# Hash attention with a feed-forward block: the order of VectorE's work between two pairs of heads, and how the second pair's q and k are turned

## Chip, cores and metric

The kernel runs on one core of a Trainium2 chip. The metric is the device time of one execution in microseconds (us). The engines are named as in the profile: PE is TensorE (matmuls; PEld its weight loads), DVE is VectorE, ACT is ScalarE, POOL is GpSimd, SP is SyncE, which only issues DMAs here.

## The reference

Inputs are q, k, v of shape (4 batches, 8 heads, 768 positions, 64), a projection of 64 x 6, and a feed-forward block of 512 x 2048 and 2048 x 512 with a slope alpha per hidden unit. For each batch and head:

```
bucket(q), bucket(k) = the 6 sign bits of q @ proj and of k @ proj
scores = q @ k.T / 8, and -1e9 where bucket(q) != bucket(k)
attn   = softmax(scores) @ v
```

The heads are put beside each other to x (3072 x 512), and the result is

```
h = x @ w_in;  g = max(h, 0) + alpha * min(h, 0);  out = g @ w_out
```

## The kernel before

**Stages.** The function `fast_path` has two stages. The attention stage works on 16 pairs of heads (`NPAIR`; two heads fill the 128 partitions), one after the other, and in its shadow converts the feed-forward weights, which come as 64-bit floats, to 32-bit ones, 32 pieces of 128 x 512, two for each pair. The feed-forward stage then runs blocks of seven products each with sums and differences on DVE. Nearly all compute instructions go through `do`, which pins them to the order of the program on their engine, so the order in the source is the order on each engine; an instruction that waits holds up all behind it. DMAs that are not wrapped in `do` may be placed among these by the framework.

**One pair on PE.** `scores(pi, ...)` makes 12 cells: each is four matmuls into a tile `sc` of two PSUM banks (the hash bits `qb`, `kb` in bf16, then `qT`, `kT` in f32), and ACT's exponential (L770) writes it to `pt`. `hash_bits(pi + 1)` then makes the next pair's bits (`hs`, ACT's sign L735, and six small DMAs from POOL, L740 and L742). `attend(pi)` multiplies `pt` by v into `av` (L800), 96 matmuls. `totals(pi)` multiplies the summed probabilities `accd` by ones into `sm` (L814), 16 matmuls. `sc`, `hs`, `sm` and the transposes `tp_q`, `tp_k` share a ring of three PSUM tiles (`two_banks`), so the third score cell of a pair takes the tile that `sm` had, when `st` has read it.

**One pair on DVE.** `add_first` (L778) sums the first two probability tiles into `accp` as soon as four exponentials are there. For the pair before come `dn` (L842) and `x` (L848), the end of `divide`. Then follow one weight's `weight_sum` (L637, L640), `weight_clamp` (L606) for the next weight, `add_third` (L786), `add_last` (L782, L783), the second weight's `weight_parts` (L612) and `weight_sum` (L637, L640), and `add_total` (L789), which adds `accp` to `accd`. Then the q and the k of pair pi + 2 are turned, in three of the pairs with a subtraction for the feed-forward block (L873) behind them, and `divide(pi)` begins: `st` (L830, two transposes of `sm`), `rc`, `rr` (L831, L833, reciprocals), `vs` (L840), and, through `weight_begin`, `weight_clamp` and `weight_parts` of the next weight and `add_first` of the next pair.

**How q and k are turned.** Pairs 2 to 15 are loaded by blocks (`load_blocks`, L512: four DMAs of 96 KB in rows of 128 B from SP for each tile), so that a 32 x 32 block transpose on DVE (`turn_blocks`, L703) gives `qT` and `kT`; ACT scales q (L1197). Pairs 0 and 1 are loaded whole (`load_part`, L501, rows of 256 B), turned by PE with an identity (`turn`, L694, six transposes each), and copied out of PSUM by ACT (q, with the scale, L699) and DVE (k, L697). The source tiles `qn` and `kn` have three buffers, `qT` and `kT` two.

**Weights.** ACT's two conversions (`weight_abs`, L596 to `wr` and L600 to `wx`) fill two buffers that `weight_sum` frees. POOL makes four differences for every four pieces (`weight_sums`, L658), each 1.27 us; a small copy of one column of `accd` (L675, `late_sum`) stands ahead of one of them and makes it wait for that tile.

Of the kernel before, what the change touches and what calls it, by code (L numbers as in the profile page):

```python
# [12 lines left out]
AF = mybir.ActivationFunctionType  # L13
# [394 lines left out]
def fast_path(  # L408
# [12 lines left out]
    nc = tc.nc  # L421
# [15 lines left out]
    DOWN = 2.0 ** -20  # L437
# [5 lines left out]
    do = tc.keep_in_program_order  # L443
    PE, DVE, ACT, POOL = nc.tensor, nc.vector, nc.scalar, nc.gpsimd
# [10 lines left out]
    NPAIR = len(pairs)  # L455
# [24 lines left out]
    nat, tr, bits = {}, {}, {}  # L480
    accp, accd, av, vsum, sums = {}, {}, {}, {}, {}

    def load(pi, name):
        b, hp = pairs[pi]
        src = {"q": q, "k": k, "v": v}[name]
        if name == "v":
            t = pool.tile([P, 2, NC * D], F32, name=f"vn{pi}", tag="vn")
            nc.sync.dma_start(t, src[b, 2 * hp : 2 * hp + 2].rearrange("h (p c) d -> p h (c d)", c=NC))
            nat[name, pi] = t
        elif pi > 1 and name in BY_BLOCKS:  # L490
            load_blocks(pi, name)
        else:
            load_part(pi, name, slice(0, NC), nc.sync)

    def load_part(pi, name, cs, queue):
        b, hp = pairs[pi]
        src = {"q": q, "k": k}[name]
        if cs.start == 0:
            nat[name, pi] = pool.tile([P, NC, 2, D], F32, name=f"{name}n{pi}", tag=f"{name}n", bufs=3)
        for s in range(2):  # L500
            queue.dma_start(nat[name, pi][:, cs, s], src[b, 2 * hp + s].rearrange("(p c) d -> p c d", c=NC)[:, cs])  # L501

    BY_BLOCKS = 'qk'

    def load_blocks(pi, name):
        b, hp = pairs[pi]
        src = {"q": q, "k": k}[name]
        nat[name, pi] = t = pool.tile([P, NC * 4, 32], F32, name=f"{name}n{pi}", tag=f"{name}n", bufs=3)
        for s in range(2):
            for h in range(2):  # L510
                a = D * s + 32 * h
                nc.sync.dma_start(  # L512
                    t[a : a + 32].rearrange("i (c u) d -> i c u d", u=4),
                    src[b, 2 * hp + s, :, 32 * h : 32 * h + 32].rearrange("(u i c) d -> i c u d", u=4, c=NC),
                )
# [62 lines left out]
    def load_weight(i):  # L578
        if i < NW:
            i = order[i]  # L580
            raw[i] = pool.tile([P, 512], moe_w_in.dtype, name=f"raw{i}", tag="raw", bufs=3)
            nc.sync.dma_start(raw[i], piece(i))
# [19 lines left out]
    def weight_clamp(i):  # L602
        if i < NW:
            i = order[i]
            x = wx[i]
            do(DVE.tensor_scalar(x, x, HI_MIN, None, op0=ALU.max, op1=ALU.max, accum_out=wmax[:, i : i + 1]))  # L606

    def weight_parts(i):
        i = order[i]
        x = wx[i].bitcast(U32)  # L610
        turned = i < HW and i % 4 == 3
        do(DVE.tensor_scalar(  # L612
            x, x, 3, 0x40000000 if turned else 0xC0000000, op0=ALU.logical_shift_left, op1=ALU.bitwise_xor,
        ))
# [55 lines left out]
    late_sum = const.tile([P, 1], F32, name="late_sum")  # L670

    def weight_sums(count, after=None):

        if sums_due and after is not None:
            do(POOL.tensor_copy(late_sum, after[:, 0, :1]))  # L675
        while sums_due and count:
            fn, x = sums_due.pop(0)
            count -= fn.__name__ == "one"
            fn(*x)


    def two_banks(name):
        return psum.tile([P, 2, 512], F32, name=name, tag="sc", bufs=3)

    BOTH = slice(0, 2)

    def turn(pi, name, halves=BOTH, engine=None):

        src = nat[name, pi].rearrange("p c h d -> p c (h d)")
        if halves.start == 0:  # L690
            tr[name, pi] = pool.tile([P, S], F32, name=f"{name}T{pi}", tag=f"{name}T")
        ps = two_banks(f"tp_{name}{pi}")
        for c in range(CH * halves.start, CH * halves.stop):
            do(PE.transpose(ps[:, c // CH, c % CH * P :][:, :P], src[:, c], ident))  # L694
        dst = tr[name, pi].rearrange("p (h w) -> p h w", h=2)[:, halves]
        if engine is DVE:
            do(DVE.tensor_copy(dst, ps[:, halves, :CW]))  # L697
        else:
            do(ACT.activation(dst, ps[:, halves, :CW], AF.Copy, scale=DOWN if name == "q" else 1.0))  # L699

    def turn_blocks(pi, name):
        tr[name, pi] = pool.tile([P, S], F32, name=f"{name}T{pi}", tag=f"{name}T")
        do(DVE.transpose(tr[name, pi], nat[name, pi].rearrange("p w d -> p (w d)")))  # L703
# [55 lines left out]
    def scores(pi, cells):  # L759
        for kc, g in cells:  # L760
            sc = two_banks(f"sc{pi}_{kc}_{g}")
            ks = slice(kc * P, (kc + 1) * P)
            qs = slice(g * CW, (g + 1) * CW)
            for what, first in ((bits, True), (tr, False)):
                for s in range(2):
                    r = slice(D * s, D * s + D)
                    do(PE.matmul(  # L767
                        sc[:, s, :CW], what["k", pi][r, ks], what["q", pi][r, qs], start=first, stop=not first,
                    ))
            do(ACT.activation(pts[kc][:, g, :, :CW], sc[:, :, :CW], AF.Exp, scale=SCALE / DOWN))  # L770


    def p(kc):
        return pts[kc].rearrange("p g s w -> p (g s) w")[:, :, :CW]

    def add_first(pi):
        accp[pi] = pool.tile([P, 2 * NCH, CW], F32, name=f"accp{pi}", tag="accp", bufs=1)
        do(DVE.tensor_tensor(accp[pi], p(0), p(1), op=ALU.add))  # L778

    def add_last(pi):  # L780
        accd[pi] = pool.tile([P, 2 * NCH, CW], F32, name=f"accd{pi}", tag="accd", bufs=1)
        do(DVE.tensor_tensor(accd[pi], p(3), p(4), op=ALU.add))  # L782
        do(DVE.tensor_tensor(accd[pi], accd[pi], p(5), op=ALU.add))  # L783

    def add_third(pi):
        do(DVE.tensor_tensor(accp[pi], accp[pi], p(2), op=ALU.add))  # L786

    def add_total(pi):
        do(DVE.tensor_tensor(accd[pi], accd[pi], accp[pi], op=ALU.add))  # L789
# [351 lines left out]
    for half in (first, second):  # L1141
        turn(0, "q", half)
        turn(0, "k", half, DVE)
        if half is first:
            nil[0]()
            hash_bits(0, first, DVE)
    load(1, "q")
    load(1, "k")
    load_weight(0)
    load(0, "v")  # L1150
    for i in range(1, 3):
        load_weight(i)
# [4 lines left out]
    ahead = [(kc, 0) for kc in range(CH)]  # L1157
    scores(0, ahead)
    hash_bits(0, second, DVE)
    turn(1, "q")  # L1160
    turn(1, "k", BOTH, DVE)

    weight_abs(0, DVE)
    weight_clamp(0)
# [1 line left out]
    for pi in range(NPAIR):  # L1166
        i = 2 * pi

        def weight_begin():
            weight_clamp(i)  # L1170
            weight_parts(i)
            add_first(pi)

        scores(pi, [c for c in CELLS if pi or c not in ahead])
        if pi:
            divide(pi - 1, weight_begin)
        else:
            add_first(pi)
        weight_sum(i)
        weight_group(i)  # L1180
        load_weight(i + 3)
        if pi == 0:
            weight_abs(1, DVE)
        weight_clamp(i + 1)
        add_third(pi)
        add_last(pi)
        weight_parts(i + 1)
        weight_sum(i + 1)
        weight_group(i + 1)
        load_weight(i + 4)  # L1190
        add_total(pi)
        if pi + 1 < NPAIR:
            hash_bits(pi + 1)
        weight_sums(1, accd[pi])
        if pi + 1 < NPAIR:
            if pi:
                do(ACT.activation(tr["q", pi + 1], tr["q", pi + 1], AF.Copy, scale=DOWN))  # L1197
        if pi + 2 < NPAIR:
            for name in "qk":
                (turn_blocks if name in BY_BLOCKS else turn)(pi + 2, name)  # L1200
        attend(pi)
        if pi + 1 == NPAIR:
            now = ff1(0, 0)
            now.step(1)
        totals(pi)
        if pi + 1 == NPAIR:
            now.step(5)
            divide(pi)
        else:
            weight_abs(i + 2)  # L1210
        if pi + 2 < NPAIR:
            load(pi + 2, "v")
        if pi in (9, 11, 15):
            load_w((9, 11, 15).index(pi))
        if pi in (9, 10, 12):
            load_x(0, *{9: (0,), 10: (2, 3), 12: (1,)}[pi])
        if 11 <= pi < 14 or pi == 15:
            sum_x(0, min(pi - 11, 3), DVE)
        if pi == 1:
            setup_alpha()  # L1220
        for name in "qk":
            magnitude(pi, name)
            if pi + 3 < NPAIR:
                load(pi + 3, name)
        if pi + 1 < NPAIR:
            weight_abs(i + 3)
# [97 lines left out]
```

## Time and profile before

| | us |
|---|---|
| median of 3 runs (880.39 to 883.41) | 880.72 |
| the profiled execution | 881.48 |
| its span, first to last instruction | 879.7 |

| engine | busy, us | share of the span | instructions |
|---|---|---|---|
| PE | 865.7 | 98% | 5718 |
| DVE | 745.3 | 85% | 1214 |
| ACT | 370.0 | 42% | 654 |
| POOL | 96.2 | 11% | 212 |

The attention stage takes the first 330 us or so, the feed-forward stage the rest. From 40 to 330 us PE is busy 285.18 of 290 us, DVE 262.09, ACT 219.71. TensorE's granted clock is 0.999 of full speed. A line of the timeline reads: start (us from the span's start), length, engine, line of the kernel, operation, output<-inputs, shape, count; in brackets is the idle time of the engine before it, and what ended it. A wait is put down to the event that came last.

### The profile page before, as it was taken

The page shows a single profiled execution, that of the slowest core. Times are in us where ns is not written, and L with a number is a line of the kernel's source. Part 1 is how long each engine was busy: PE and PEld are TensorE (multiplying, and loading weights), DVE is VectorE, ACT ScalarE, POOL GpSimd, SP SyncE. Part 2 cuts the span into 40 slices and gives each one's busy share as a digit, 9 for nine tenths or more (in the row PEclk, how much of TensorE's full clock was granted, in tenths as well). Part 3 has the DMA queues.
Part 4 walks back from the last instruction along what each step waited for, and adds up shares of the span by engine and source line. Part 5 has one row for each costly group of instructions (what it writes and reads, how often), then busy time and mean ns, then how long its engine had stood idle before and what let it go on. Part 6 is the DMA issues. An engine that isn't in the chain of part 4 may idle for free.

```text
span 879.7 us, 15201 instructions
## 1 busy us (share of the span) xinstructions
PE 865.7 (98%) x5718; PEld 576.0 (65%) x5718; DVE 745.3 (85%) x1214; ACT 370.0 (42%) x654; POOL 96.2 (11%) x212
## 2 busy tenths in 40 slices
PE   9999999999999999999999999999999999999996
PEld 4444444444444445559996558996557997557996
DVE  5999988999999878899897769898668989668986
ACT  7877788888877652221112222112222112222111
POOL 1221322213313301120000000000000000000000
PEclk9999999999999999999999999999999999999999
DMA  8866797798897617685433425334434433520242
GB/s 205 182 144 138 182 217 179 143 236 224 204 260 161 212 42 263 207 301 222 139 129 88 172 88 200 112 119 119 141 122 155 140 119 91 184 85 1 96 152 68
DMA packets 167682, 137.22 MB, mean 156 GB/s; under 512 B 122880, under 2 KB 151248, under 8 KB 164016
## 3 DMA queue, kind: packets, MB, share of 16 engines
q1 hardware_dynamic: 160000, 123.64, 49.9%
q0 software_dynamic: 5184, 11.34, 3.9%
q10 hardware_dynamic: 2416, 1.18, 0.5%
q8 instruction: 47, 0.77, 0.4%
q14 instruction: 35, 0.29, 0.1%
HBM read 104.87 MB, written 28.31 MB: 151 GB/s over the span
## 4 chain that ended last, share of the span: by engine, by line
PE 66%; DVE 19%; issue 5%; DMA 4%; ACT 3%; SPq 1%; DVEq 0%; ACTq 0%
PE sc L767 3%; ACT pt L770 3%; DVE accd L789 3%; PE f_0a L901 2%; PE z_4a L901 2%; PE z_7a L901 2%; PE z_3a L901 2%; PE z_6a L901 2%; PE z_5a L901 2%; PE f_4a L901 2%; PE f_3a L901 2%; PE f_2a L901 2%; PE f_1a L901 2%; DVE accd L782 2%; DVE accp L786 2%
## 5 line engine op out<-in xcount | busy, mean ns | idle before, releaser
L770 ACT ACTIVATE pt<-sc 128x768 f32<-128x768 f32 x192 | 155.0, 811 | 37.0 <-PE sc L767 37.0
L767 PE MATMUL sc<-qT,kT 64*128 64x384 f32 x768 | 155.2, 482 | 0.0
L800 PE MATMUL av<-pt,vn 128*32 128x385 f32 (+1 forms) x1536 | 127.4, 486 | 0.0
L800 PEld LDWEIGHTS av<-pt,vn 128*32 128x32 f32 x1536 | 48.8, 109 | 77.4 <-issue 68.0
L767 PEld LDWEIGHTS sc<-qT,kT 64*128 64x128 f32 x768 | 68.2, 187 | 37.8 <-issue 36.4
L954 DVE TENSOR_TENSOR g<-g,g 128x384 f32<-128x384 f32 x128 | 68.4, 555 | 2.2
L767 PE MATMUL sc<-qb,kb 64*128 64x384 bf16 x384 | 63.3, 323 | 1.7 <-DVE st L830 1.4
L1018 DVE TENSOR_TENSOR gs<-g,gs 128x768 f32<-128x768 f32 x56 | 53.3, 952 | 1.0
L1010 DVE TENSOR_TENSOR ws<-wl 128x512 f32<-128x512 f32 x56 | 38.5, 687 | 18.4 <-DMA wl<-w_out_s 16.1
L1018 DVE TENSOR_TENSOR gs<-g 128x768 f32<-128x768 f32 x56 | 53.3, 952 | 0.0
L778 DVE TENSOR_TENSOR accp<-pt,pt 128x1536 f32<-128x1536 f32 x16 | 28.3, 1770 | 21.2 <-ACT pt L770 21.2
L740 POOL DMA_DIRECT2D qb<-kb x60 | 30.1, 505 | 136.0 <-ACT kb L735 114.8
L950 DVE SCALAR_TENSOR_TENSOR g<-h,alpha 128x384 f32<-128x384 f32 x32 | 19.7, 616 | 25.2 <-ACT h L943 25.1
L767 PEld LDWEIGHTS <-kb 64*128 64x128 bf16 x384 | 19.0, 94 | 31.6 <-DVE st L830 5.3
L596 ACT ACTIVATE wr<-raw 128x512 int32<-128x512 uint32 x32 | 22.5, 703 | 26.8 <-issue 19.5
L783 DVE TENSOR_TENSOR accd<-accd,pt 128x1536 f32<-128x1536 f32 x16 | 28.1, 1759 | 1.7
L786 DVE TENSOR_TENSOR accp<-accp,pt 128x1536 f32<-128x1536 f32 x16 | 28.0, 1753 | 0.0
L782 DVE TENSOR_TENSOR accd<-pt,pt 128x1536 f32<-128x1536 f32 x16 | 28.0, 1752 | 0.0
L789 DVE TENSOR_TENSOR accd<-accd,accp 128x1536 f32<-128x1536 f32 x16 | 28.0, 1751 | 0.0
L901 PE MATMUL f_0a<-x,wi 128*128 128x384 f32 x64 | 23.5, 489 | 0.0
L901 PE MATMUL f_4a<-x,wi 128*128 128x384 f32 x64 | 23.3, 486 | 0.0
L901 PE MATMUL f_1a<-x,wi 128*128 128x384 f32 x64 | 23.3, 486 | 0.0
(353 smaller groups left out, 1742.8 us busy)
## 6 DMA issues: line engine op xcount, KB each, us to landing
wi<-w_in_s SPq DMA_DIRECT2D x32, 896.0 KB, 4.7
wl<-w_out_s SPq DMA_DIRECT2D x16, 1024.0 KB, 4.8
wl<-w_out_r SPq DMA_DIRECT2D x12, 1024.0 KB, 5.1
raw<-in_moe_w_out_dram SPq DMA_DIRECT2D x16, 512.0 KB, 4.6
raw<-in_moe_w_in_dram SPq DMA_DIRECT2D x16, 512.0 KB, 4.3
w_in_s<-wsi SPq DMA_DIRECT2D x16, 448.0 KB, 6.3
vn<-in_v_dram SPq DMA_DIRECT2D x16, 384.0 KB, 5.2
x_s<-x SPq DMA_DIRECT2D x16, 384.0 KB, 2.6
```

Source lines behind the costliest of these rows:

```text
L740: nc.gpsimd.dma_start(bits["q", pi][D * s : D * s + 32, cols], raw[c + 32 : c + 64, 2 * half])
L767: do(PE.matmul(sc[:, s, :CW], what["k", pi][r, ks], what["q", pi][r, qs], start=first, stop=not first,))
L770: do(ACT.activation(pts[kc][:, g, :, :CW], sc[:, :, :CW], AF.Exp, scale=SCALE / DOWN))
L778: do(DVE.tensor_tensor(accp[pi], p(0), p(1), op=ALU.add))
L782: do(DVE.tensor_tensor(accd[pi], p(3), p(4), op=ALU.add))
L786: do(DVE.tensor_tensor(accp[pi], accp[pi], p(2), op=ALU.add))
L789: do(DVE.tensor_tensor(accd[pi], accd[pi], accp[pi], op=ALU.add))
L800: do(PE.matmul(av[pi][D * s + t : D * s + t + 32, g, :w], nat["v", pi][:, s, kc * D + t : kc * D + t + 32], pts[kc][:, g, s, :w], start=(k ...
L901: do(PE.matmul(self.ps[bank], self.left(left, k), self.right(right, k), start=start and k == 0, stop=k == self.nk - 1, skip_group_check=no ...
L954: do(DVE.tensor_tensor(new_g(b, to)[:, i], g_m[b, x][:, i], g_m[b, y][:, i], op=ALU.subtract))
L1010: do(DVE.tensor_tensor(t, w2[b, n, x], w2[b, n, y], op=op))
L1018: do(DVE.tensor_tensor(t, g2[b, n, x], g2[b, n, y], op=ALU.subtract))
```

## The change

- `add_total(pi)` stands directly behind `add_last(pi)`, ahead of the second weight's `weight_parts` and `weight_sum`.
- Of the two turns at the end of a pair only q's stays; k's turn of pair pi + 1 stands in `weight_begin`, so behind the reciprocals and `vs` of `divide(pi - 1)` and ahead of `weight_clamp`.
- POOL's delayed weight difference waits for `qT` of pair pi + 2 instead of `accd`, and in the last two pairs for nothing.
- Pair 1 is loaded by blocks and turned by DVE like the later ones: q's four DMAs come from SP, k's four from POOL. ACT's scaling of q now happens for pair 1 too, with its own instruction.

On the engines this means: PE has 12 transposes less. The first of POOL's four new DMAs stands between the two instructions that make the identity, the other three behind POOL's memsets. On DVE the copy L697 of pair 1 becomes two instructions of L703.

```
@@ load
-        elif pi > 1 and name in BY_BLOCKS:
+        elif pi and name in BY_BLOCKS:
@@ load_blocks
-    def load_blocks(pi, name):
+    def load_blocks(pi, name, queue=nc.sync):
...
-                nc.sync.dma_start(
+                queue.dma_start(
@@ weight_sums
-            do(POOL.tensor_copy(late_sum, after[:, 0, :1]))
+            do(POOL.tensor_copy(late_sum, after[:, :1]))
@@ the start
-    load(1, "k")
+    load_blocks(1, "k", nc.gpsimd)
...
-    turn(1, "q")
-    turn(1, "k", BOTH, DVE)
+    turn_blocks(1, "q")
+    turn_blocks(1, "k")
@@ the loop over the pairs
         def weight_begin():
+            if pi + 1 < NPAIR:
+                turn_blocks(pi + 1, "k")
             weight_clamp(i)
...
         add_last(pi)
+        add_total(pi)
         weight_parts(i + 1)
         weight_sum(i + 1)
         weight_group(i + 1)
         load_weight(i + 4)
-        add_total(pi)
         if pi + 1 < NPAIR:
             hash_bits(pi + 1)
-        weight_sums(1, accd[pi])
-        if pi + 1 < NPAIR:
-            if pi:
-                do(ACT.activation(tr["q", pi + 1], tr["q", pi + 1], AF.Copy, scale=DOWN))
+            do(ACT.activation(tr["q", pi + 1], tr["q", pi + 1], AF.Copy, scale=DOWN))
         if pi + 2 < NPAIR:
-            for name in "qk":
-                (turn_blocks if name in BY_BLOCKS else turn)(pi + 2, name)
+            turn_blocks(pi + 2, "q")
+            weight_sums(1, tr["q", pi + 2])
+        else:
+            weight_sums(1)
         attend(pi)
```

## The prediction

> **What bounds the kernel now.** I read the page first, for the engine that is never free.
>
> ```profile
> PE 865.7 (98%) x5718; PEld 576.0 (65%) x5718; DVE 745.3 (85%) x1214; ACT 370.0 (42%) x654; POOL 96.2 (11%) x212
> ```
>
> TensorE (PE) has 14 us of idle time in all, so the change can gain little: it must take PE's waits away, or PE's work. The table of waits of PE names them (total us, times, longest):
>
> ```profile
> PE sm L814 <- DVE accd L789: 3.4, 14, 0.3
> PE sc L767 <- DVE st L830: 1.4, 3, 0.5
> ```
>
> Both lie in the attention stage and both are VectorE (DVE) arriving late. The timeline shows one of the 14 (start, us, engine, line, out<-in, count):
>
> ```profile
> 93.74 1.76 DVE L778 TENSOR_TENSOR accp<-pt,pt 128x1536 f32<-128x1536 f32 x1 [1.38 <-ACT pt L770]
> ...
> 104.53 3.42 PE L800 MATMUL av<-pt,vn 128*32 128x384 f32 x40
> 107.12 0.13 PEld L800 LDWEIGHTS av<-pt,vn 128*32 128x32 f32 x4 [0.19 <-issue]
> 106.28 1.75 DVE L789 TENSOR_TENSOR accd<-accd,accp 128x1536 f32<-128x1536 f32 x1
> 107.95 0.97 DVE L703 STREAM_TRANSPOSE qT<-qn 128x768 f32<-128x768 f32 x1
> 108.18 0.86 PE L814 MATMUL sm<-accd,ones 128*32 128x192 f32 x16 [0.23 <-DVE accd L789]
> 108.97 0.34 PE L767 MATMUL sc<-qb,kb 64*128 64x384 bf16 x2
> 113.33 1.76 DVE L778 TENSOR_TENSOR accp<-pt,pt 128x1536 f32<-128x1536 f32 x1 [1.39 <-ACT pt L770]
> ```
>
> This is a closed loop: from L778 to the end of L789 14.29 us of DVE work without a wait (93.74 to 108.03), 0.15 to the sums' first matmul, 0.79 to the next scores, 4.36 until ScalarE (ACT) has the fourth exponential: 19.59 us, the period. So DVE's chain, not PE's work, sets the period. Pair 0 is the control:
>
> ```profile
> 25.56 4.38 PE L800 MATMUL av<-pt,vn 128*32 128x384 f32 x52
> 27.64 1.75 DVE L789 TENSOR_TENSOR accd<-accd,accp 128x1536 f32<-128x1536 f32 x1
> 29.12 0.13 PEld L800 LDWEIGHTS av<-pt,vn 128*32 128x32 f32 x4 [0.19 <-issue]
> 29.76 0.84 PE L814 MATMUL sm<-accd,ones 128*32 128x192 f32 x16
> 30.53 0.34 PE L767 MATMUL sc<-qb,kb 64*128 64x384 bf16 x2
> ```
>
> Its accd is ready at 29.39, 0.37 before sm. From the last weight load of av to sm it takes 0.64 us; in the pair above 1.06. A wait of 0.23 thus costs 0.42, since the overlap with av's tail is lost too.
>
> **What the Trainium skill says.** "TensorE: Matmul & The Clock Gate", section "Step-by-step: what each phase is for": only weight loads are pulled ahead, matmuls stay in program order. The trace agrees: the 16 matmuls of sm hold up the next pair's scores behind them. "DMA: Bandwidth & Descriptors", section "Issuing engines are not separate DMA queues": DMAs of all issuers share the same 16 engines and interleave. It agrees: from 2 to 4 us ACT's queue took 62.1% of them and SP's 43.3%.
>
> **Part 1: L789 moves ahead of L612, L637, L640.** These three take 1.79 us (first start 45.58, L789's start 47.37 in pair 1). accd is ready 1.79 us earlier, 1.4 us or more ahead of need; 14 waits go. Per pair 0.42, less 0.02 (sm to scores is 0.77 in pair 0, 0.79 here): 14 x 0.40 = **-5.6 us**. Upper bound 0.46 (pair 0's weight load of sm, idle 0.26 before it, may itself have lost 0.07), lower 0.24 (the plain wait). What is late next: PE's own work, since DVE keeps about 1 us of its 1.38 idle per pair. Behind L789 stand the weight's second pass and, waiting for it, ACT's second weight conversion: it began at 204.38, right after L640, and left ACT idle 2.30 before the first exponential at 208.00. With L640 1.67 later and scores 0.40 earlier, 2.30 - 1.67 - 0.40 leaves 0.23 us. I count zero; the score ring of three banks covers some half a microsecond more (first exponential 0.81, fourth cell 2.4 after the first). SP's raw load for that slot issues 1.7 later with the loads behind it; the weight is read in the next pair and v's loads later still: zero.
>
> **Part 2: k's turn moves behind the reciprocals.** In pairs 11 to 13 a subtraction for x (L873) also stands ahead of st:
>
> ```profile
> 246.81 0.92 DVE L873 TENSOR_TENSOR x<-x,x 128x768 f32<-128x768 f32 x1
> 247.64 0.64 DVE L830 STREAM_TRANSPOSE st<-sm 128x192 f32<-128x192 f32 x2
> 248.34 0.34 PE L767 MATMUL sc<-qb,kb 64*128 64x384 bf16 x2 [0.47 <-DVE st L830]
> ```
>
> The third score cell needs the bank that st frees; these periods are 20.23 instead of 19.58 (sm at 225.70, 245.28, 265.51). kT's pitch ahead of st is 0.86 (245.95 to 246.81); st comes that much earlier, scores 0.40: 0.86 - 0.40 = 0.46 of the 0.65 goes, 3 x 0.46 = **-1.4 us** (bounds 0.9 and 2.0). k's 0.9 us now fall where DVE waited 1.38 for ACT: free, and its first reader (the hash at the end of the scores) is 8 us away. If that cover were gone it would push L778 by up to 0.9. Its data was loaded a pair earlier, so no DMA wait is added. GpSimd's weight difference now waits for qT, about 0.9 later than before relative to the pair's sums; it takes 1.27 and rr's copies 0.9, and dn needs them only 4 us on: zero.
>
> **Part 3: pair 1 by VectorE.** Gone: 12 transposes of PE and a copy of 0.81 on ACT, and DVE's copy of 0.96; added: two DVE turns (0.97 + 0.94) and a scaling on ACT (0.84) later, where ACT is idle. The transposes cost PE little:
>
> ```profile
> 12.10 0.88 PE L694 MATMUL tp_q<-ident,qn 128*128 128x128 f32 x6
> 12.25 1.17 ACT L748 ACTIVATE qb<-hsq,hb 32x384 bf16<-32x384 f32 x2
> 13.81 0.34 PE L767 MATMUL sc<-qb,kb 64*128 64x384 bf16 x2 [0.17 <-DVE kb L754]
> 14.28 0.68 ACT L596 ACTIVATE wr<-raw 128x512 int32<-128x512 uint32 x1
> ```
>
> The next scores need both qb, done at 13.42, so only 13.81 - 13.42 = 0.4 can be gained. Against it stand the loads. By blocks a tile is 3072 packets of 128 B instead of 1536 of 256 B. From 18 to 20 us (128 B) 1517 packets took 90.3% of 16 engines, 19.0 ns each; from 6 to 8 us (256 B) 1428 took 78.5%, 17.6 ns. A tile takes 3.65 instead of 1.69 us, both +3.9. Free DMA time from 4 to 8 us is 0.36 x 2 + 0.215 x 2 = 1.15. k comes over GpSimd (POOL): 8 DMAs of 512 rows took 759 ns, 60 of 32 rows 505, so 768 rows are about 0.9 each. The first is placed between ident's two instructions (ident 1.32 to 2.2, needed at 4.38: covered), three after the memsets, to 6.4. The first meets q's and k's first halves, which PE awaits at 4.38 (bounds 0 and 0.8, I take 0.5), the others q's second half, awaited at 7.47 (same bounds, 0.5). The qb of above then ends at 14.4. The first weight (issued 7.91, landing 4.9 later, 12.8) lands between 12.8 and 12.8 + 3.9 - 1.15 = 15.6; ACT's wr stands ahead of the next exponential, which moves from 14.87 to 15.1 or, at worst, 16.3. Three banks of scores absorb part: **+0.5 us** (bounds -0.4 and +2.0). On DVE the two turns end about 16.5 and accd of pair 0 about 29.0, against a need at 30: covered.
>
> **Sum.** -5.6 - 1.4 + 0.5 = -6.5. The profiled execution took 881.48 (span 879.7 and 1.8 around it): 875.0 after. It stood 0.76 above the median of 880.72, so the median becomes **874.2 us**. The feed-forward stage keeps its instructions and shifts.
>
> **Rivals.** (a) PE regains only the plain waits, 3.4 + 1.4, and the start costs 1.5: 877.4. For it: 0.42 rests on one pair as control. Against: that pair has the same instructions. Chance 0.11. (b) ACT becomes the loop: its margin of 0.23 is thin, and if the second conversion is some 1 us later than worked out, 0.3 of each pair's 0.40 is lost: -6.5 + 14 x 0.3 = -2.3, 878.4. Against: its input landed early in all but one pair. 0.05. (c) Slower: k of pair 1 lands late from GpSimd's queue. DVE is in order; the turn of k stands ahead of all weight and sum work of pair 0. Landing by 15.6 is free, to 16.8 absorbed by accd's slack, from there each microsecond delays the end by one; past 23.3 the gain is gone. Issued by 6.4, with the longest landing of this queue before (11.9) it would be 18.3, 875.7. To end at 886 it must land near 28. For it: no such short rows on this queue in this trace. Against: its 1536 B packets took as long as the others' of that size. 0.05. (d) That L789 isn't moved where the diff says: the program order is pinned on each engine and the built order shows it ahead in all pairs; nil.
>
> **Numbers.** The main case, 0.79, spans 880.7 - 8.8 = 871.9 (14 x 0.46 + 3 x 0.65 + 0.4) to 880.7 - 5.0 = 875.7. With (a) the range is 871.9 to 877.4. About 0.5% (4.4 us, below 876.3) can be told from no change: faster 0.79, same 0.16 (a, b), slower 0.05.
>
> **What would show it.** Right: no wait of sm for accd; sm some 0.64 after av's last weight load; periods near 19.2, of pairs 11 to 13 near 19.4; kT between vs and the clamp with DVE's idle before L778 near 1.0; scores at 14 to 14.5 after qb, not after kb. Wrong: idle of ACT's exponentials put down to ACT itself; DVE's first turn idle on a DMA of kn; PE's first transposes after 5.2; periods still at 19.5.

## The result, and the profile after

| | before | after |
|---|---|---|
| median of 13 runs each, us | 881.15 (880.24 to 883.41) | 878.43 (877.71 to 881.05) |
| ratio, 95% interval | | 0.9970 (0.9961 to 0.9979) |

The change gained 0.3%, 2.7 us; 874.2 was predicted, and 878.43 lies outside the range of 871.9 to 877.4. The profiled execution of after took 881.05 (span 879.3), 2.6 above its median; near pair 12 it has a wait of 2.7 us, shown below.

The page of after, busy time, share and instructions of each engine:

```profile
PE 863.8 (98%) x5706; PEld 576.9 (66%) x5706; DVE 757.9 (86%) x1215; ACT 366.9 (42%) x654; POOL 99.4 (11%) x215
```

PE has its 12 transposes less. The odd entry is DVE: 12.6 us more than before for one instruction more. The two turns of pair 1 in place of a copy are about 1 us of it (0.97 + 0.94 - 0.96). Most of the rest lies in two lines that the change doesn't touch: L831 takes 8.6 us in all instead of 2.8, L612 18.9 instead of 13.6. The table of PE's waits (total us, times, longest):

```profile
PE sc L767 <- ACT pt L770: 2.7, 1, 2.7
PE sc L767 <- DVE st L830: 2.2, 4, 1.3
...
PE sc L767 <- ACT qb L748: 1.0, 2, 0.7
```

The 14 waits of `sm` for `accd` are gone, as predicted. The waits for `st` were to shrink from 1.4 us, and grew to 2.2; the first line is a new wait. DVE's own table shows what the additional busy time was paid with. Before:

```profile
DVE accp L778 <- ACT pt L770: 21.2, 16, 2.0
```

After:

```profile
DVE accp L778 <- ACT pt L770: 7.6, 8, 2.3
```

Before, DVE was idle here in every pair, 1.3 us on average; now it is in half of them. The timeline of after from 86 us, in the same pair as in the prediction, shows where it went:

```profile
87.42 0.84 PE L814 MATMUL sm<-accd,ones 128*32 128x192 f32 x16
...
87.73 0.97 DVE L703 STREAM_TRANSPOSE qT<-qn 128x768 f32<-128x768 f32 x1
...
88.62 0.60 DVE L830 STREAM_TRANSPOSE st<-sm 128x192 f32<-128x192 f32 x2
...
88.98 1.27 POOL L658 TENSOR_TENSOR wsi<-wsi 128x512 f32<-128x512 f32 x1
...
89.26 1.01 DVE L831 TENSOR_SCALAR rc<-st 128x12 f32<-128x12 f32 x1
...
91.45 0.64 DVE L606 TENSOR_SCALAR_CACHE_REDUCE wx<-wx 128x512 f32<-128x512 f32 x1
...
91.72 1.28 POOL L658 TENSOR_TENSOR wsi<-wsi 128x512 f32<-128x512 f32 x1
...
92.14 1.14 DVE L612 TENSOR_SCALAR wx<-wx 128x512 uint32<-128x512 uint32 x1
...
93.20 1.75 DVE L778 TENSOR_TENSOR accp<-pt,pt 128x1536 f32<-128x1536 f32 x1
```

L831 handles 12 numbers a partition and took 0.17 us before; here it takes 1.01 and ends at 90.27, just when GpSimd's weight difference ends (88.98 + 1.27 = 90.25). L612 took 0.42 and takes 1.14 beside the second difference. Together this is 1.56 us, and L778 now starts with no idle before it. The second meeting has no edit of GpSimd behind it: L612 now stands behind k's turn, and so runs later; in k_back below, with that turn back, it takes 0.42 everywhere. In the kernel before, the first difference ran beside transposes and the second, after L612, in DVE's idle time:

```profile
88.74 1.28 POOL L658 TENSOR_TENSOR wsi<-wsi 128x512 f32<-128x512 f32 x1
...
89.27 0.93 DVE L703 STREAM_TRANSPOSE kT<-kn 128x768 f32<-128x768 f32 x1
...
90.12 0.60 DVE L830 STREAM_TRANSPOSE st<-sm 128x192 f32<-128x192 f32 x2
...
90.76 0.17 DVE L831 TENSOR_SCALAR rc<-st 128x12 f32<-128x12 f32 x1
...
91.93 0.43 DVE L612 TENSOR_SCALAR wx<-wx 128x512 uint32<-128x512 uint32 x1
...
92.49 1.27 POOL L658 TENSOR_TENSOR wsi<-wsi 128x512 f32<-128x512 f32 x1
```

The Trainium skill describes this, and the prediction missed it: "SBUF — State Buffer", section "Who interferes with whom", says that VectorE and GpSimd share one pair of ports as an exclusive lock, that `tensor_scalar` in its two-port modes (not the form with an accumulator) and operations with two SBUF inputs contend for it, that the later one blocks for the whole instruction of the other, and that an operation with one SBUF input outside these modes doesn't. What this case shows agrees: `tensor_scalar` L831 0.17 to 1.01, until the difference ends; transposes of 0.93 and 0.60 beside a difference, no longer than elsewhere; L606, the accumulating form, 0.64 although the second difference starts beside it, and that difference its usual 1.28. Operations with two SBUF inputs are held up in the experiments below. In which mode an instruction ran, no trace shows.

The starts of the sums (L814 in the timeline) give the periods. The differences (16 in all, two in each of eight pairs) come in two pairs running, here from 87.42 to 125.83; the periods from 87.42 on are 19.14, 19.27 and 19.71 (before, 19.59 each). I read this so: DVE falls behind by what its idle time doesn't pay; the lead of `accd` over `sm` covers it at first, and the third period pays. From 242.14 on they are 20.58, 24.11 and 19.15. The 24.11 holds the other new wait:

```profile
267.21 0.67 ACT L596 ACTIVATE wr<-raw 128x512 int32<-128x512 uint32 x1 [7.57 <-DMA raw<-in_moe_w_out_dram]
...
268.34 3.12 ACT L770 ACTIVATE pt<-sc 128x768 f32<-128x768 f32 x4
...
269.19 0.34 PE L767 MATMUL sc<-qb,kb 64*128 64x384 bf16 x2 [2.74 <-ACT pt L770]
```

One raw weight (512 KB) lands at 267.2, and the exponentials stand behind its conversion. Its load was issued at 259.49 and took 7.6 us; from 242 to 262 us the packets fill 1.00 of the 16 DMA engines' time. In the kernel before (0.96 in the same stretch) the same load was issued at 258.57, landed 5.65 us later, at 264.22, and was converted from 264.33 in an idle stretch of ACT. So the computing around the load comes 2.8 us earlier (sums at 262.72 instead of 265.51), the issue does not, and this execution's transfer is 2 us slower on top.

### The profile page after: what moved, and what is told of

Read it like the earlier page. It is cut to its first block, busy times and chain, and to the rows that moved or that the text cites. A ratio compares the mean times of both kernels' runs of the same rounds, so it can differ in the third digit from the quotient of the medians.

```text
span 879.3 us, 15198 instructions
## 1 busy us (share of the span) xinstructions
PE 863.8 (98%) x5706; PEld 576.9 (66%) x5706; DVE 757.9 (86%) x1215; ACT 366.9 (42%) x654; POOL 99.4 (11%) x215
## 4 chain that ended last, share of the span: by engine, by line
PE 67%; DVE 11%; issue 3%; ACT 2%; DMA 2%; SPq 0%; DVEq 0%; ACTq 0%
PE sc L767 4%; PE av L800 4%; PE f_0a L901 2%; PE z_4a L901 2%; PE z_7a L901 2%; PE z_3a L901 2%; PE z_6a L901 2%; PE z_5a L901 2%; PE f_4a L901 2%; PE f_2a L901 2%; PE f_1a L901 2%; PE f_3a L901 2%; PE z_2a L901 2%; PE f_5a L901 2%; PE z_1a L901 2%
## 5 line engine op out<-in xcount | busy, mean ns | idle before, releaser
L770 ACT ACTIVATE pt<-sc 128x768 f32<-128x768 f32 x192 | 153.1, 811 | 6.0 <-PE sc L767 5.2
L778 DVE TENSOR_TENSOR accp<-pt,pt 128x1536 f32<-128x1536 f32 x16 | 28.1, 1754 | 7.6 <-ACT pt L770 7.6
L901 PE MATMUL f_0a<-x,wi 128*128 128x384 f32 x64 | 23.5, 489 | 0.0
L901 PE MATMUL f_1a<-x,wi 128*128 128x384 f32 x64 | 23.3, 486 | 0.0
L901 PE MATMUL f_2a<-x,wi 128*128 128x384 f32 x64 | 23.3, 486 | 0.0
```

The lines of the kernel that those rows point to most:

```text
L901: do(PE.matmul(self.ps[bank], self.left(left, k), self.right(right, k), start=start and k == 0, stop=k == self.nk - 1, skip_group_check=no ...
```

## Experiments

Three theories. **A**: GpSimd's differences hold up VectorE; the change put them there. **C**: the DMA queue can't follow, and a raw weight arrives late near pair 12. **E**: the parts of the change are not worth the figures that they were given: with part 1 alone the wait only moves on to `st`, or the start (part 3) costs more. (B and D in the expectations are the rivals of A and C.) For each experiment the median of its 4 to 21 runs, the range and the ratio to the kernel before on the same chip are given. Three chips were used, one for each group; the medians of before were 881.10, 881.14 and 881.63.

### diff_shifted: the differences moved beside transposes

```
-            weight_sums(1, tr["q", pi + 2])
+            weight_sums(1, made[0])        # made[0]: the second weight's sum, L640
...
+        weight_sums(1, r[:, 0, :1])        # in divide: the second difference waits for rc
         for q0 in (0, D):                  # the copies of rr
...
-        weight_sums(1)                     # where it stood, behind the copies
```

> The changed kernel, with GpSimd's weight differences (L658) moved: the first waits for the second weight's sum instead of qT, so it runs beside the turn of q and st; the second stands ahead of the four copies of rr, so it runs beside the turn of k. Nothing is left out. Theory A (GpSimd's differences hold up VectorE's small tensor_scalar instructions, and VectorE's lost time is what keeps the periods at 19.7): L831 goes back from a mean of 536 ns to about 173, L612 from 591 to about 424, the periods of the pairs with differences go from 19.1 to 19.7 down to 19.15, and the stretch from the first to the eleventh sum (193.2 us after, 196.0 before) becomes about 191.6. Rival B (VectorE's chain is just too long after the change, GpSimd has no part): durations and periods stay. The total: 877 if the stretch's gain comes through, 878.4 if a late weight load near pair 12 takes it back (theory C).

Measured: 876.07 (875.98 to 878.26), ratio 0.9946 (0.9932 to 0.9959). The views of the line of `rc` (minimum, median and maximum in ns), first of after, then of this run:

```profile
L831 DVE TENSOR_SCALAR rc<-st x16: 173/352/1082, 31.8 to 327.5; 128x12 f32<-128x12 f32 x16
```

```profile
L832 DVE TENSOR_SCALAR rc<-st x16: 173/173/198, 32.2 to 324.5; 128x12 f32<-128x12 f32 x16
```

Its timeline in the same pair:

```profile
88.48 1.28 POOL L659 TENSOR_TENSOR wsi<-wsi 128x512 f32<-128x512 f32 x1
...
89.65 0.17 DVE L832 TENSOR_SCALAR rc<-st 128x12 f32<-128x12 f32 x1
...
90.10 1.28 POOL L659 TENSOR_TENSOR wsi<-wsi 128x512 f32<-128x512 f32 x1
...
92.94 1.76 DVE L779 TENSOR_TENSOR accp<-pt,pt 128x1536 f32<-128x1536 f32 x1 [0.79 <-ACT pt L771]
```

With the collisions gone DVE has its idle again (0.79 of the "about 1 us" predicted), and the periods from 68.66 to 240.98 are 19.14 or 19.15, every one. A is shown for its part: 2.4 us of the missing 4.2 (net, since in two pairs the moved difference meets the subtraction, as shown below). Only the three periods with the subtraction, which end with the sums of pairs 12 to 14, are still longer (19.50, 22.13, 20.29); the profiled execution, at 878.26 the slowest of its five, has the late raw weight too.

### before_pool_kT: the collision put into the kernel before

```
-        weight_sums(1, accd[pi])
...
+        weight_sums(1, tr["k", pi + 2] if pi + 2 < NPAIR else None)   # behind both turns
         attend(pi)
```

> The kernel before, with one edit: GpSimd's second weight difference of a pair waits for k's turn instead of for accd, so that it runs beside st, rc and the clamp on VectorE instead of beside the two turns. If GpSimd holds up VectorE's tensor_scalar through the shared port, L831 goes from 173 ns to about 1000 in the eight pairs with a difference; VectorE's idle of 1.38 us before accp pays for it (about 0.3 left) and the time stays within 1 us of 881. If the stretch in the kernel after had another cause (its own order of instructions), L831 stays at 173 everywhere.

Measured: 885.94 (885.90 to 886.67), ratio 1.0056 (1.0042 to 1.0070): 4.8 us slower. L831's part of the expectation held (0.71 to 1.07 us in the eight pairs with a difference), the time within 1 us of 881 did not. Its timeline in a pair with a difference:

```profile
109.94 1.26 POOL L658 TENSOR_TENSOR wsi<-wsi 128x512 f32<-128x512 f32 x1
...
110.29 0.94 DVE L831 TENSOR_SCALAR rc<-st 128x12 f32<-128x12 f32 x1
...
112.79 1.28 POOL L658 TENSOR_TENSOR wsi<-wsi 128x512 f32<-128x512 f32 x1
...
113.27 2.41 DVE L778 TENSOR_TENSOR accp<-pt,pt 128x1536 f32<-128x1536 f32 x1 [0.61 <-ACT pt L770]
```

L831's 0.77 more is paid by the idle time, 1.38 before and 0.61 here, as expected. But the second difference comes later too and now holds up L778 (two SBUF inputs, 1.76 to 2.41), which stands behind that idle time: 0.65 more on the path, and the period, from 108.12 to 128.36, is 20.24 instead of 19.59. One edit of GpSimd's wait, with nothing changed on VectorE, thus makes a kernel 0.56% slower.

### total_alone and k_back: is each part worth its figure?

total_alone is the kernel before with the one line `add_total(pi)` moved, as in part 1:

```
         add_last(pi)
+        add_total(pi)
         weight_parts(i + 1)
...
-        add_total(pi)
```

> The kernel before, with only the total of the sums (L789) moved ahead of the second weight's passes; k's turn, GpSimd's wait and pair 1 stay as before. The prediction's step taken literally: 14 waits of sm go, 0.40 us each, 875.5. Theory E (st ends when it did, because it stands behind the same work of VectorE, and frees the bank of the third score cell; so the wait moves from sm to the third cell): sm earlier by 0.4, but a wait of about 0.4 for st at L767 in every pair, total 880.5 to 881.5. With theory A on top, GpSimd's difference now runs beside L612 in 8 pairs and delays st there by up to 0.8: up to 885.

Measured: 888.54 (887.29 to 889.03), ratio 1.0083 (1.0069 to 1.0097), slower by 7.4 us, more than the 885 at which the expectation ended. From its timeline, in a pair with the meeting and, last, in one without:

```profile
86.81 1.28 POOL L658 TENSOR_TENSOR wsi<-wsi 128x512 f32<-128x512 f32 x1
...
86.84 1.80 DVE L637 SCALAR_TENSOR_TENSOR wx<-raw,wx 128x512 uint32<-128x512 uint32 x1
...
91.04 0.61 DVE L830 STREAM_TRANSPOSE st<-sm 128x192 f32<-128x192 f32 x2
...
91.70 0.34 PE L767 MATMUL sc<-qb,kb 64*128 64x384 bf16 x2 [1.28 <-DVE st L830]
...
208.56 0.69 DVE L637 SCALAR_TENSOR_TENSOR wx<-raw,wx 128x512 uint32<-128x512 uint32 x1
```

The difference waits for `accd`, which is earlier now, and meets L637 (0.69 to 1.80). And `st` stands behind both turns, while scores come earlier: PE's table has `sc` waiting for `st` 12 times, 11.9 us. The periods of this trace part the two: from 68.39 to 249.76 us the five behind a meeting are 20.59 to 20.69, the four without one 19.48 to 19.58 (before, 19.58 or 19.59). So the order alone gains next to nothing, and a meeting costs 1.1, which is what L637 is held up. As a second way to part them, k_back is after with k's turn back ahead of `st`; its difference runs beside that turn and holds nothing up, but for two pairs in which it meets the subtraction L873 (0.92 to 1.64 and 1.51):

```
-            if pi + 1 < NPAIR:
-                turn_blocks(pi + 1, "k")
             weight_clamp(i)
...
             turn_blocks(pi + 2, "q")
+            turn_blocks(pi + 2, "k")
```

> The kernel after with k's turn back behind q's turn, ahead of st; GpSimd's difference still waits for q's turn and so runs beside k's turn, where nothing is held up. If total_alone was slow because of collisions with L637 alone, this has none: L831 stays at 173 ns, and the time is 879 to 881 us. If the order alone is enough (st is then about 0.9 us too late for the third score cell in every pair, since the sums come 0.4 earlier and st doesn't), scores wait for st in most pairs, about 0.5 to 0.9 us each, periods of 19.5 or more, 883 to 888 us.

Measured: 883.24 (883.00 to 885.11), ratio 1.0022 (1.0013 to 1.0031), at the lower edge of what the second theory gave. L831 is 173 ns in its median (218 at most), yet the periods from 69.43 to 245.33 us are 19.47 to 19.64. Its timeline:

```profile
108.39 0.84 PE L814 MATMUL sm<-accd,ones 128*32 128x192 f32 x16
...
110.55 0.60 DVE L830 STREAM_TRANSPOSE st<-sm 128x192 f32<-128x192 f32 x2
...
111.21 0.34 PE L767 MATMUL sc<-qb,kb 64*128 64x384 bf16 x2 [0.26 <-DVE st L830]
```

`sm` no longer waits for `accd`, but the third score cell waits for `st`, here 0.26. As in the prediction a short wait costs more than its length: the period is 19.58 instead of 19.15. So the order alone takes nearly all of part 1's gain: parts 1 and 2 are worth something only together.

### pair1_by_pe and shift_pe1: the start

pair1_by_pe is after with pair 1 loaded whole and turned by TensorE, as before (part 3 undone); shift_pe1 adds diff_shifted's edit.

```
...
-    load_blocks(1, "k", nc.gpsimd)
+    load(1, "k")
...
-    turn_blocks(1, "q")
-    turn_blocks(1, "k")
+    turn(1, "q")
+    turn(1, "k", BOTH, DVE)
...
```

> The changed kernel, with pair 1 loaded whole and turned by PE as before. The prediction put pair 1's change at +0.5 us (bounds -0.4 and +2.0), so this should be 0.5 faster than the changed kernel, 877.9. By the two profiles the first sum moved by only 0.06 (29.76 to 29.82), so by that 878.4 and no difference that can be told.

> The kernel after with two edits: GpSimd's weight differences moved beside transposes (as in diff_shifted) and pair 1 loaded whole and turned by TensorE (as in pair1_by_pe). If the two losses are separate (port collisions in eight pairs; late first scores at the start), they add: 878.4 - 2.4 - 0.8 = 875.3 us, the first sums near 29.4 and the periods of pairs 2 to 11 at 19.15. If what follows is only handed on to the wait for the raw weight near pair 12, nothing of the start's 0.8 is kept and it stays at 876.1; the wait for pt near pair 12 then grows by about 0.8 over that of diff_shifted.

Measured: pair1_by_pe 877.66 (877.42 to 878.34), ratio 0.9962 (0.9949 to 0.9976), 0.8 below after with overlapping intervals; its first sums begin at 29.38 instead of 29.82. The first sums differ from one execution to the next by some tenths, but the two starts can be told apart: 28.99 to 29.76 in the seven profiles with pair 1 turned by TensorE, 29.82 to 30.29 in the seven with it turned by VectorE, 0.64 later on average. shift_pe1 876.75 (875.75 to 878.05), ratio 0.9951 (0.9938 to 0.9965): not 875.3, so the two don't add here. Its runs are spread over 2.3 us, which pointed to a wait that differs from run to run.

### w_later, w_13, shift_pe1_w13: the late raw weight

The second feed-forward weight (`wi`, 896 KB) is loaded by SP in pair 11, next to that raw weight. w_later (from after) issues it in pair 14, w_13 (from after) and shift_pe1_w13 (from shift_pe1) in pair 13:

```
-        if pi in (9, 11, 15):
-            load_w((9, 11, 15).index(pi))
+        if pi in (9, 13, 15):
+            load_w((9, 13, 15).index(pi))
```

> The changed kernel, with the second of the three early loads of feed-forward weights (896 KB, load_w(1)) issued after pair 14 instead of pair 11. Nothing is left out. Theory C (near pair 12 the DMA engines are 99% busy, so a raw weight lands late, ScalarE waits for it ahead of the exponentials, 7.6 us in the profile after, and the pairs' gain is given back): ScalarE's wait for the raw weight falls below 4 us, PE's 2.7 us wait for an exponential in pair 12 goes, the period of 24.1 becomes about 19.7, the total 875 to 877. Rival D (the wait is a chance of the one profiled execution): the total stays at 878.4 and other profiles of the changed kernel don't show it.

> The kernel after with one edit: the second feed-forward weight's load is issued in pair 13 instead of pair 11. If the raw weight that lands late near pair 12 costs after about what the same edit took off shift_pe1 (1.5 us), it gives 876.9 us, and its runs lie closer together than after's (877.7 to 881.1), since the size of that wait is what varies. If VectorE, which has no idle left in after, sets the pace in pairs 11 to 13 in any case, the time stays at 878.4.

> As shift_pe1, but the second feed-forward weight's load (896 KB) is issued in pair 13 instead of pair 11, away from the stretch where SP's DMAs keep the 16 engines 99% busy. If the late raw weight near pair 12 is a matter of that traffic, its wait goes (period of pair 12 from about 22 to below 20.5) and, unlike in w_later, the last pair's sign copies on GpSimd's queue are not met: 873.5 us, 1.5 to 2 under shift_pe1. If moving 896 KB only moves the collision, the loss reappears in pairs 13 to 15 as waits of scores for qb<-kb or for raw, and the time is that of shift_pe1 or up to 2 us more.

Measured: w_later 880.25 (879.66 to 881.50), ratio 0.9988 (0.9982 to 0.9995); w_13 878.27 (878.06 to 878.48), ratio 0.9961 (0.9948 to 0.9975); shift_pe1_w13 875.22 (874.99 to 875.70), ratio 0.9932 (0.9919 to 0.9946). In w_later PE's wait for `pt` near pair 12 is gone, but the 875 to 877 expected did not come, since the last pair pays:

```profile
305.21 0.33 PE L767 MATMUL sc<-qb,kb 64*128 64x384 bf16 x1 [0.55 <-DMA qb<-kb]
...
305.88 0.32 PE L767 MATMUL sc<-qb,kb 64*128 64x384 bf16 x1 [0.34 <-DMA qb<-kb]
```

From the fifteenth sums to the feed-forward stage's first matmuls (L901) it takes 20.1 us there and 18.5 in after; these two waits are 0.9 of the difference, and ACT's wait for a raw weight is now there (5.9 us, until 305.76). In pair 13 the load meets neither: ACT's table in w_13 has no wait for a raw weight (11.9 us in after), its 5 runs lie within 0.4 us, the 13 of after within 3.3. Yet the median of w_13 is after's. C is thus a matter of some executions, the profiled one among them, and not of after's median. From shift_pe1, where computing is further ahead, the same edit took 1.5 us of the median (not all that was expected: 873.5); that this was the late weight is not shown there, since the profiled execution of shift_pe1 doesn't have the wait.

### x_later, best_x, shift_x_w13: the subtraction for x

In shift_pe1_w13 three periods are still too long, 19.54, 20.21 and 20.15. Its timeline in the last:

```profile
280.75 1.27 POOL L659 TENSOR_TENSOR wsi<-wsi 128x512 f32<-128x512 f32 x1
...
281.28 1.56 DVE L874 TENSOR_TENSOR x<-x,x 128x768 f32<-128x768 f32 x1
...
282.76 0.63 DVE L831 STREAM_TRANSPOSE st<-sm 128x192 f32<-128x192 f32 x2
```

The subtraction (two SBUF inputs) stands ahead of `st` and, with the difference at its new place, meets it: 0.92 becomes 1.56. The edit moves it behind the clamp's two passes in the next turn of the loop, ahead of `add_first`:

```
             weight_parts(i)
+            if 12 <= pi < 15:
+                sum_x(0, pi - 12, DVE)
             add_first(pi)
...
-        if 11 <= pi < 14 or pi == 15:
+        if pi == 15:
...
```

x_later is after with it, best_x is shift_pe1_w13 with it, and shift_x_w13 is best_x with pair 1 turned by VectorE as in after.

> The kernel after with one edit: the subtraction for x of pairs 11 to 13 (0.92 us on VectorE, ahead of st) moves behind the clamp's two passes, ahead of the first exponentials' addition. If st behind it is what lengthens those three periods (20.6, 24.1 and 19.15 in after's trace, the second one raised by a raw weight), the first of them falls to about 19.7, the port collision's level, and the whole gains about 1 us: 877.4. If VectorE has no idle there, the 0.92 is only moved within a full engine and the time stays at 878.4 within 0.4.

> shift_pe1_w13 with the same move of the subtraction for x. VectorE has 0.8 us of idle a pair here, so the subtraction is nearly covered; the periods of pairs 12 to 14, 19.54, 20.21 and 20.15, fall to about 19.25, and the time from 875.2 to 872.9 us. If something else than st sets these three periods (ACT's exponentials behind a raw weight), they stay above 19.8 and the time is 874.5 to 875.2.

> best_x without the edit at the start: pair 1 comes by blocks and is turned by VectorE, as in after. With the late weight and the subtraction out of the way nothing later should hide the start, so the difference to best_x is what part 3 of the change costs: first sums 30.2 instead of 29.55, 0.65 us, 873.5. If part 3 costs nothing that reaches the end, both have the same time within 0.3 us.

Measured: x_later 878.90 (878.55 to 879.33), ratio 0.9969 (0.9957 to 0.9981), nothing gained. The first of the three periods did fall, from 20.57 in w_13 to 19.71, as expected, but the three that follow (20.07, 20.46 and 20.46, in w_13 19.50, 20.35 and 20.07) took it back: where DVE has no idle, the 0.92 is only handed on. best_x **872.97** (872.91 to 872.99), ratio **0.9900 (0.9885 to 0.9916)**. shift_x_w13 873.85 (873.35 to 875.38), ratio 0.9914 (0.9901 to 0.9928), so part 3 of the change costs 0.9; the first sums begin at 29.24 in best_x and at 29.90 in shift_x_w13. From best_x's timeline:

```profile
276.89 0.42 DVE L612 TENSOR_SCALAR wx<-wx 128x512 uint32<-128x512 uint32 x1
...
278.04 0.13 PEld L815 LDWEIGHTS sm<-accd,ones 128*32 128x32 f32 x4 [0.19 <-issue]
...
278.36 0.84 PE L815 MATMUL sm<-accd,ones 128*32 128x192 f32 x16
...
282.62 0.94 DVE L874 TENSOR_TENSOR x<-x,x 128x768 f32<-128x768 f32 x1
...
282.78 0.83 POOL L839 COPY rr<-rr 32x12 f32<-32x12 f32 x1
```

From the first sums to the fifteenth all its periods are 19.14 to 19.19 but one (19.31), and PE's table has no wait for `st`, `accd` or `pt` left. L612 takes its 0.42 again, and `sm` starts without a wait. The last two lines show the meeting from the other side: GpSimd's copy, 0.19 alone, takes 0.83 behind the subtraction.

## Why the prediction was wrong, by its own steps

The sums' starts divide the miss. The profiled execution of w_13 (span 876.3) is after without the disturbed stretch. Against a span of before of 879.7 it gains 3.4, where 6.5 were worked out:

| stretch, us | predicted | w_13 | miss |
|---|---|---|---|
| start to the third sums (69.02 before), change | +0.5 - 0.8 = -0.3 | -0.5 | -0.2 |
| nine periods, 68.53 to 242.38 | 9 x 19.19 = 172.7 | 173.85 | +1.1 |
| three periods, 242.38 to 302.79 | 3 x 19.4 = 58.2 | 60.41 | +2.2 |
| fifteenth sums to the end (573.5 before) | 573.5 | 573.5 | 0 |

The other 1.1 of the 4.2 lies between executions: the prediction took 0.76 off to come to a median of three runs, which with more runs was 0.4 higher, and after's median stands 0.4 above this execution.

**Right, with part 2 beside it: what bounds the kernel, and part 1's 0.40 a pair.** Where nothing collides, the period goes from 19.59 to 19.15, 0.44; the wait of 0.23 did cost the overlap as well. Rival (a), the plain waits only, is out. Rival (b), ACT as the loop, gave the time that was measured, 878.4, but by coincidence: in after's collision pair L778 starts without idle, so DVE and not ACT is late there.

**Wrong: part 2, "GpSimd's weight difference now waits for qT ... zero".** This is the step that failed. It asked when the difference's readers need it, and not what runs on VectorE meanwhile. The shift was larger, too, than the 0.9 worked out: the difference starts 1.56 behind the sums in after (88.98 and 87.42), 0.14 in before (88.74 and 88.60). The answer was in the trace of before, where both differences lie beside transposes or idle time. With it fell part 1's "DVE keeps about 1 us of its 1.38 idle per pair": true in diff_shifted (0.79), false in after (none in eight of the 16). In place of zero it cost 2.4 us of the median (after against diff_shifted).

**Wrong for the same reason: part 2's -1.4 in pairs 11 to 13.** The step has `st` 0.86 earlier against the sums, and did not ask whether DVE can carry the subtraction's 0.92 at all. It can, nearly, if there is idle time: in diff_shifted and shift_pe1_w13 the first of the three periods, in which the subtraction runs alone, is 19.50 and 19.54, near the 19.4 worked out. In w_13 DVE enters the first behind from two collision pairs (20.57), and the other two have collisions of their own (19.50, 20.34). The first period parts the two: with the subtraction alone it is 0.4 above 19.15, with the two collision pairs alone (x_later, 19.71) 0.56, with both 1.42, since the same idle time can't pay twice. x_later also shows that the subtraction's place alone gains nothing then; best_x, that with the collisions and the late weight away it costs nothing: all three periods are 19.14 or 19.15.

**Wrong in its division: parts 1 and 2 as separate terms.** k_back is 4.8 above after, though it has none of the meetings with L831 and L612: k's turn is not worth 1.4 in three pairs, it carries part 1 in all of them. "What is late next: PE's own work" was true of both together; with part 1 alone `st` is next. The sum was not hurt by it, but whoever makes part 1 alone loses 0.8%, with the meetings that come with it.

**Too confident: "SP's raw load ... zero".** Its reader was said to be a pair away. Near pair 12 that margin is used up, and the wait took 2.7 us in the profiled execution. That this is traffic is likely, not settled: with the 896 KB moved, the wait is gone from the trace and the 5 runs lie closer together, but 10 of after's 13 runs lie within 1 us as well. It explains little of the median.

**Right in size, in part by luck: part 3, +0.5.** It is 0.9 between medians and 0.66 between first sums. `sc` waits for `qb`, as described, but the terms did not come as worked out: PE's first transposes are not late (4.32, before 4.41; 0.5 was put there), the second ones are 0.9 late (8.39, before 7.47; 0.5 was put there), and `qb` ends at 13.83, not 14.4. Rival (c), k late from GpSimd's queue, did not happen.

With the collisions, the late weight and the subtraction out of the way, shift_x_w13, which keeps all three parts, took 873.85, close to the 874.2 predicted; but it has help that after has not, so this does not make the prediction right. Of the 4.6 us between it and after, 2.4 are the places of the differences. The other 2.2 come with the moves of the load and of the subtraction, which made alone from after gave 0.2 and nothing.

## What to carry to other kernels

When an edit changes what a GpSimd instruction waits for, or moves VectorE's instructions against it, write down which VectorE instructions will run beside it, and charge every `tensor_scalar` and every operation with two SBUF inputs there with the rest of GpSimd's instruction. In these runs transposes and idle time were the places for it. Then ask whether the idle time that is to pay stands behind the instruction held up, or ahead of it. And if VectorE's busy time rises with the same instructions, look at the maxima of its small operations first: 173/352/1082 ns told the story at once.

## What the runs showed of the hardware

The price of a meeting follows what is left of the partner's instruction, not the size of the operation held up: L831 with 12 elements a partition lost 0.84 us to a difference of 1.27, L637 with 512 elements 1.11. Each time it was about 0.15 less than what was left when the held-up instruction started: L831 0.84 of 0.99, L612 0.72 of 0.86, L637 1.11 of 1.25, L778 0.65 of 0.80. It works both ways (GpSimd's copy 0.19 to 0.83). And GpSimd, 11% busy, moves the time of a kernel in which TensorE is 98% and VectorE 86% busy: shifting its 16 differences alone is worth between -2.4 us (diff_shifted) and +4.8 us (before_pool_kT).
